# A gated linear attention with a low-rank mixer on one Trainium2 core: first-layer products per chunk, neighbouring chunks' products in joined pieces, and the written order that goes with them

## The chip, the core and the metric

One core of a Trainium2 chip runs the whole program. TensorE multiplies (results go to PSUM), VectorE (DVE), ScalarE (ACT) and GpSimd (POOL) work element by element, and the sync engine (SP) issues most transfers. Each engine works through its own queue in order. The time is device time in microseconds of one execution; shown is the median of three runs, 530.83 us (529.35 to 532.6). One more execution was profiled; all rows of the profile are from it.

## What is computed

Inputs are q, k, v and a complex gate a for 4 batches, 8 heads, 768 steps and 48 channels per head. With the gate's magnitude limited to 0.999, each head keeps a complex state of 48x48:

```python
S = a[t] * S + outer(k[t], v[t])          # a, S complex; k, v real
y[t] = q[t] @ real(S)
```

The heads' y side by side are x (768 x 384 per batch). A mixer follows:

```python
h = (x.T @ U @ V).T                       # over the 768 steps, rank 32
u = x + h
out = u + maximum(u @ w_ch1, 0) @ w_ch2   # 384 -> 1536 -> 384
```

## The kernel before

**Tiling.** The 768 steps of a batch are cut into 6 chunks of 128, so there are 24 chunks, numbered through all batches; two neighbouring chunks are a group for the gates and a pair (`m`) for the mixer. Within a chunk, prefix sums of log magnitude and phase (products with a triangular matrix, lines 777 to 848) turn the recurrence into ordinary products. `prep` weighs q and k with the decays and phases and turns them: up to chunk 5 on TensorE, later by a transfer that transposes.

**A chunk's chain** (`chain`, lines 940 to 1025) has these pieces on TensorE: `products` (L956), k against q, in two halves of 64 steps; `state` (L976), k against v, the chunk's contribution to the state, in two pieces of four heads; `inside` (L1005), the masked k-q products against v; `before(0)` and `before(1)` (L1013), q against the state that came in and against that of the middle. VectorE copies the products through a mask into `AT` (L959) and makes the states `GM` (middle) and `G` (end) from the state products. ScalarE copies the results out to `xo` (L1022, L1024). `state` and `inside` use the array as tiles of 64 by 64; `products` and `before` as tiles of 64 columns over all rows; the mixer's products use the whole array.

**The mixer** (`mixer`) of pair 0 is done partly ahead: its first layer is made from x before the low-rank part is known (`turned`, `up`, 36 products of 256 columns), and `corrected` adds the low-rank part later with weights `more` that come from `ranked` (r is turned, L1116; multiplied with w1, L1124; copied to `more` by ScalarE, L1128). Pair 0's second layer is `down` (L1303), pair 1's first layer `up` (L1102); from pair 2 on the first layer is done with fewer products (`up_fewer`, L1214), and from pair 1 on the second too (`down_two`, L1346). `spread` (L1071) multiplies r with V, `mixed` adds it to xo, `turned` transposes xo into `uT` (L1087, L1091).

**The gates** of a group need the tables for logarithm and exponential first and those for arctangent and sine then; each change is a table load on ScalarE (L463). From chunk 7 on, the phase at the end of a chunk is added to the first row of the next chunk's by a transfer with addition that POOL issues (L828, `gate<-F`); the cast L836 on VectorE waits for it, and the product L842 for the cast.

**The order.** Each piece is entered into a plan with its engine, what it reads and writes, and which buffers it takes. The program is then issued in the order of the list `ORDER`, written out by hand as numbers of the pieces; the plan asserts that no piece comes before what it needs and that no buffer is taken too early. A piece is issued as a whole: nothing of the same engine comes between its instructions. `WARM` puts filler products (L1513, units of 128 columns into a tile that nothing reads) ahead of numbered pieces; before, 33 of them with 52 units. `SPARE` puts single products of 128 columns (L1506) ahead of pieces, into the bank that the piece will overwrite.

**Banks.** Five PSUM banks are shared in rotation by all pieces tagged T or Y: a piece that takes a bank waits until the reader of the bank's last contents is done. State products take two (one for the last chunk of a batch), `inside` and `before` two more.

Weights come as 64-bit numbers and are converted in pieces by VectorE and ScalarE (lines 616 to 625, `stage` and `w`), while the attention part runs.

## Time and profile before

| | |
|---|---|
| median of three runs | 530.83 us |
| profiled execution | 529.77 us |
| its span, first to last instruction | 528.0 us |
| TensorE products busy | 509.3 us (96%), 6670 records |
| VectorE busy | 414.5 us (79%) |
| ScalarE busy | 346.0 us (66%) |
| mean granted TensorE clock | 0.997 |

The span is what the trace shows; 1.77 us of the execution lie around it. A product of 32-bit floats has two records for TensorE (PE) and two for its weight load (PEld), so 12 records are six products. The chain of waits follows the work that ended last back to its start; in it, a row's time runs to the start of what follows, while a row of the timeline runs to the modelled end of its last instruction, which overlaps the next. A wait row gives who waited for whom, the total, how often, and the longest. A row of windows gives the window, its length, then busy time and number of instructions for TensorE, its weight loads, VectorE, ScalarE and GpSimd, the granted clock, the share of the transfer engines and the rate.

### The profile page before, as it was taken

To read this page: it belongs to the slowest core of one execution; us is meant where nothing else is said; L and a number is where in the kernel's file an instruction comes from. 1 tells how busy PE (TensorE), PEld (TensorE's weight loads), DVE (VectorE), ACT (ScalarE), POOL (GpSimd) and SP (SyncE) were. 2 spreads that over 40 slices of the span, in tenths; PEclk is the share of its full clock that TensorE was granted. 3 is DMA by queue.
4 is the path that set the end of the run, shared out by engine and by line. 5 is a ranking of instruction groups with operands and counts; after the bars stand their busy time and mean duration, and the time that the engine had idled before them with its cause. 6 is when DMAs were issued, how large, how long until landed. Compare 5 with 4: busy or idle time off the path is not lost.

```text
span 528.0 us, 15692 instructions
## 1 busy us (share of the span) xinstructions
PE 509.3 (96%) x6670; PEld 460.3 (87%) x6670; DVE 414.5 (79%) x787; ACT 346.0 (66%) x555; POOL 31.6 (6%) x61
## 2 busy tenths in 40 slices
PE   4999999899999999999999999999999999999996
PEld 2777887666998997999999989999999989999996
DVE  4779897799989987898798797878796575958452
ACT  8899998998869978978896768843543313131100
POOL 1000000001010000101011000110000000000110
PEclk9999999999999999999999999999999999999998
DMA  9959958479999998999899958999897543333101
GB/s 226 173 115 270 209 115 191 140 138 217 197 215 244 216 215 145 204 217 202 205 198 227 210 144 175 170 242 229 192 217 178 108 90 61 76 60 61 39 32 35
DMA packets 280670, 87.06 MB, mean 165 GB/s; under 512 B 271288, under 2 KB 272784, under 8 KB 280592
## 3 DMA queue, kind: packets, MB, share of 16 engines
q1 hardware_dynamic: 278384, 81.63, 76.0%
q0 software_dynamic: 2208, 4.35, 2.4%
q8 instruction: 54, 0.88, 0.7%
q14 instruction: 24, 0.20, 0.1%
HBM read 43.03 MB, written 23.63 MB: 126 GB/s over the span
## 4 chain that ended last, share of the span: by engine, by line
PE 88%; ACT 5%; DMA 3%; DVE 2%; issue 1%; SPq 0%; ACTq 0%
PE down L1346 25%; PE few L1214 14%; PE bank L1214 11%; PE up L1102 6%; PE inner L956 4%; PE bank L1013 4%; PE bank L976 4%; PE down L1303 3%; PE bank L1005 2%; DMA gate<-F 2%; PE bank L1071 2%; PE bank L1087 2%; ACT gate L466 1%; PE bank L777 1%; PE bank L782 1%; PE bank L842 1%
## 5 line engine op out<-in xcount | busy, mean ns | idle before, releaser
L466 ACT ACTIVATE gate<-gate 128x768 f32<-128x768 f32 (+2 forms) x85 | 86.1, 1018 | 25.8 <-DMA gate<-in_a_im_dram 14.7
L1346 PE MATMUL down<-w,h 128*128 128x192 f32 x396 | 70.4, 328 | 0.0
L466 ACT ACTIVATE QK<-QKC 128x768 uint16<-128x768 uint16 (+1 forms) x72 | 58.5, 848 | 13.1 <-DVE QKC L469 7.9
L1346 PEld LDWEIGHTS down<-w,h 128*128 128x128 f32 x396 | 64.6, 190 | 1.2 <-issue 0.8
L469 DVE TENSOR_TENSOR QKC<-qk,cs 128x768 f32<-128x768 f32 x48 | 44.9, 952 | 1.0 <-ACT cs L466 0.6
L472 DVE TENSOR_TENSOR xo<-down,xo 128x192 f32<-128x192 f32 (+1 forms) x79 | 29.9, 385 | 14.3 <-PE down L1346 14.1
L1222 ACT COPY h<-few 128x512 f32<-128x512 f32 x35 | 20.2, 583 | 27.8 <-PE few L1214 27.6
L1222 ACT COPY h<-bank 128x512 f32<-128x512 f32 x25 | 14.3, 588 | 36.0 <-PE bank L1214 31.0
L1346 PE MATMUL down<-stage 128*128 128x192 f32 x198 | 37.2, 328 | 0.0
L1102 PE MATMUL up<-uT,w 128*128 128x256 f32 x144 | 33.8, 383 | 0.0
L1346 PEld LDWEIGHTS down<-stage 128*128 128x128 f32 x198 | 32.5, 190 | 0.3 <-issue 0.2
L1102 PEld LDWEIGHTS up<-uT,w 128*128 128x128 f32 x144 | 26.7, 190 | 4.9 <-issue 0.6
L1290 POOL DMA_DIRECT2D out_dram<-xo x32 | 18.5, 590 | 202.9 <-DVE xo L472 164.5
L463 ACT ACT_TABLE_LOAD x22 | 28.2, 1283 | 1.1 <-PEq L1567 0.7
L828 POOL DMA_DIRECT2D gate<-F x15 | 12.0, 797 | 274.7 <-DVE stage L616 86.3
L1226 DVE CUSTOM_DVE_ANT_1 h<-few,h 128x512 f32<-128x512 f32 x31 | 21.0, 686 | 8.8 <-PE few L1214 8.1
L1214 PE MATMUL few<-extra,w 128*128 128x128 f32 x216 | 27.8, 275 | 0.0
L956 PE MATMUL inner<-QK 112*64 112x64 f32 x768 | 27.5, 224 | 0.2 <-DVE AT L959 0.2
L466 ACT ACTIVATE cs<-F 128x384 f32<-128x384 f32 x48 | 24.4, 518 | 3.9 <-DVE F L851 3.7
L956 PEld LDWEIGHTS inner<-QK 112*64 112x64 f32 x768 | 24.5, 138 | 2.4 <-issue 0.8
L1214 PEld LDWEIGHTS few<-extra,w 128*128 128x128 f32 x216 | 26.3, 192 | 0.1
L466 ACT ACTIVATE es<-bank 128x384 f32<-128x384 f32 x44 | 18.4, 502 | 9.2 <-PE bank L777 8.2
(185 smaller groups left out, 1166.8 us busy)
## 6 DMA issues: line engine op xcount, KB each, us to landing
xd<-QK SPq DMA_DIRECT2D x36, 512.0 KB
gate<-in_a_re_dram SPq DMA_DIRECT2D x48, 192.0 KB
gate<-in_a_im_dram SPq DMA_DIRECT2D x48, 192.0 KB
stage<-in_moe_w_ch_dram SPq DMA_DIRECT2D x12, 768.0 KB
qk<-in_q_dram SPq DMA_DIRECT2D x24, 192.0 KB
qk<-in_k_dram SPq DMA_DIRECT2D x24, 192.0 KB
VP<-in_v_dram SPq DMA_DIRECT2D x24, 192.0 KB
out_dram<-xo POOLq DMA_DIRECT2D x12, 192.0 KB, 4.2
```

The source lines that it names most:

```text
L463: ACT(1.37, rank, lambda: nc.scalar.preload_act_table_set(name), writes=[TABLE])
L466: return nc.scalar.activation(out=o, in_=i, func=f, **kw)
L469: nc.vector.tensor_tensor(out=o, in0=a, in1=b, op=OP.mult)
L472: nc.vector.tensor_tensor(out=o, in0=a, in1=b, op=OP.add)
L956: nc.tensor.matmul(out=get(*ps0)[r:r + HC, h], lhsT=k_of(h, r, HC), rhs=q_of(h, r, HC), start=True, stop=True, tile_position=(0, r))
L976: nc.tensor.matmul(out=get(*dk[r])[x:x + D, h], lhsT=get(*ks)[at, h, x // DP, 0:D], rhs=get(*VPi)[at, h], start=True, stop=True, tile_posi ...
L1013: nc.tensor.matmul(out=get(*y[u])[side(r, u), p], lhsT=q_of(h, r * HC, HC), rhs=get(*(mid_G if r else ("G", i - 1)))[:, h], start=False, s ...
L1102: nc.tensor.matmul(out=get(*ps)[:, e], lhsT=w1[:, f, (ff + e) * 128:(ff + e + 1) * 128], rhs=get(*uT)[:, f], start=(f == 0), stop=(f == KD ...
L1214: nc.tensor.matmul(out=get(*ps)[:, q], lhsT=w()[:, q * 128:(q + 1) * 128], rhs=v[0](), start=(n == 0 and q == 0), stop=True, skip_group_ch ...
L1222: ACT(c_act(n3 * CH) - 0.045, RU, lambda i=i, k=k: nc.scalar.copy(out=at(i, k), in_=get(*ps)), [ps], [o])
L1226: DVE(c_dve(n3 * CH), RU, lambda i=i, k=k: nc.vector._custom_dve(dve_ops.TENSOR_ADD_SAT, out=at(i, k), in0=get(*ps), in1=at(i, k), s0=math ...
L1346: nc.tensor.matmul(out=get(*to)[:, part], lhsT=x(j), rhs=y[:, j], start=(first and j == 0), stop=(j == KH - 1), skip_group_check=not first)
```

## The change

There are four parts.

1. Pair 0's first layer is made for each of its two chunks by itself (`up_one`): 72 products of 128 columns for 36 of 256, in 12 pieces as before, with six evacuations of 512 columns as before. Chunk 0's pieces no longer need chunk 1.
2. From `JOIN = 8` on, the chains of neighbouring chunks of a batch are joined, at 14 places. One piece holds all state products of chunk i and the `inside` products of chunk i-1; the next holds the `before` products of chunk i-1 and `products` of chunk i. The end state `G` of chunk i is made behind the second piece, then the masked copy of chunk i and the copies out of chunk i-1. The last chunk of a batch has its `inside` and `before` in pieces of their own. 54 pieces fall away; no product does.
3. `spread` no longer lists a read of `uT`, and `turned` takes the buffer instead.
4. The order is written anew for the new numbers, on all engines. Among other things more of TensorE's work stands between a carry's transfer and its cast at ten of fifteen chunks, the loads of the second gate group stand earlier in SP's queue and the second block of weights later. There are 39 filler products with 55 units and 7 spare products for 4.

The list of the order is cut to its first lines.

```diff
--- before
+++ after
 ORDER = (
-    5, 97, 96, 0, 1, 2, 3, 102, 99, 101, 103, 4, 104, 105, 106, 107, 98, 116, 100, 115, 117, 118, 119, 10, 154, 8, 111, 112, 16, 9, 230, 108, 231,
...
+    5, 97, 96, 0, 1, 2, 3, 4, 99, 102, 101, 103, 104, 105, 106, 107, 100, 8, 98, 111, 10, 151, 230, 231, 153, 9, 154, 108, 109, 115, 116, 112, 117,
...
 )
 SPARE = {
-    410: 3, 447: 1,
+    403: 1, 447: 1, 451: 2, 636: 3,
 }
 
 WARM = {
-    112: (2, 1), 126: (1,), 136: (2, 2, 2, 2, 2, 2, 1), 141: (2,), 162: (2, 2, 2), 235: (2, 2, 2, 2, 1), 242: (2,), 245: (2,), 259: (2, 2, 1), 266: (1, 1, 1, 1, 1, 1, 1, 1, 1),
+    125: (2, 1), 136: (2, 2, 2, 2, 2, 2), 140: (2, 2), 166: (2, 2), 187: (2,), 239: (2, 2, 2, 2, 1, 1, 1, 1, 1, 1, 1, 1, 1), 242: (1, 1, 1, 1, 1, 1, 1, 1, 1, 1, 1, 1, 1),
 }
 
...
@@ -369,6 +367,7 @@
     PARTS = [[(n, n + 1) for n in range(GC)]] + [[g] for g in GROUPS[1:]]
     NG = len(GROUPS)
     AGAIN = range(NG)
+    JOIN = 8
 
     EARLY, SPREAD = 6, (0, 1, 2)
     SPLIT = range(3, NG)
@@ -948,51 +947,44 @@
             return get(*QK)[0:DQ, 1, h * CH + lo:h * CH + lo + n]
 
         ps0 = ("inner", i)
-        psum(ps0, "A", [128, H, HC])
+        last = c == NCH - 1
+        joined, joins = c > 0 and i >= JOIN, not last and i + 1 >= JOIN
+        G, mid_G = ("G", i), ("GM", i)
+        ks, dk = ("qkc", 2 * i + 1), [("dk", (i, r)) for r in range(2)]
+        parts_k = range(1 if last else 2)
+        y, xi = [("y", (i, r)) for r in range(2)], ("xo", i)
+        y_in = [VPi, ATi, mid_G] + ([("G", i - 1)] if c else [])
 
         def products():
             for h in range(H):
                 for r in range(0, CH, HC):
                     nc.tensor.matmul(out=get(*ps0)[r:r + HC, h], lhsT=k_of(h, r, HC), rhs=q_of(h, r, HC), start=True, stop=True,
                                      tile_position=(0, r))
-        PE(0.947, RL, products, [QK], [ps0], takes=[ATi], way=1, steps=4 * H)
-        DVE(0.17 + 0.00104 * H * HC, RL, lambda: nc.vector.copy_predicated(
-            out=get(*ATi), mask=mask.bitcast(I32).unsqueeze(1).to_broadcast([128, H, HC]), data=get(*ps0)), [ps0, ("mask", 0)], [ATi])
-
-        G, mid_G, last = ("G", i), ("GM", i), c == NCH - 1
-        ks, dk = ("qkc", 2 * i + 1), [("dk", (i, r)) for r in range(2)]
-        buffer(mid_G, "GM", 2, [DQ, H, D])
-        if not last:
-            buffer(G, "G", 2, [DQ, H, D])
-        parts_k = range(1 if last else 2)
-        for r in parts_k:
-            psum(dk[r], "Y", [128, H, D], [128, H, DP])
-
-        def state(h0):
-            for h in range(h0, h0 + HH):
+
+        def kept():
+            DVE(0.17 + 0.00104 * H * HC, RL, lambda: nc.vector.copy_predicated(
+                out=get(*ATi), mask=mask.bitcast(I32).unsqueeze(1).to_broadcast([128, H, HC]), data=get(*ps0)), [ps0, ("mask", 0)], [ATi])
+
+        def state(h0, n=HH):
+            for h in range(h0, h0 + n):
                 for r in parts_k:
                     at = slice(r * HC, (r + 1) * HC)
                     for x in (0, DP):
                         nc.tensor.matmul(out=get(*dk[r])[x:x + D, h], lhsT=get(*ks)[at, h, x // DP, 0:D], rhs=get(*VPi)[at, h],
                                          start=True, stop=True, tile_position=(r * HC, x))
-        for h0 in (0, HH):
-            PE(0.443, RR, lambda h0=h0: state(h0), [ks, VPi], [dk[r] + (h0,) for r in parts_k], way=3,
-               steps=4 * HH * len(parts_k),
-               takes=[mid_G] + ([] if last else [G]))
 
         half0, half1 = (lambda r=r: get(*dk[r])[0:DQ] for r in range(2))
-        if c:
-            DVE(c_dve(DM), RR, lambda: add(get(*mid_G), get("G", i - 1), half0()), [("G", i - 1), dk[0]], [mid_G])
-        else:
-            ACT(c_act(DM), RR, lambda: nc.scalar.copy(out=get(*mid_G), in_=half0()), [dk[0]], [mid_G])
-        if not last:
-            DVE(c_dve(DM), RR, lambda: add(get(*G), get(*mid_G), half1()), [mid_G, dk[1]], [G])
-            DVE(c_dve(DM), RR, lambda: mul(get(*G), get(*G), T_of(i)), [("T", group_of(i))], [G])
-
-        y, xi = [("y", (i, r)) for r in range(2)], ("xo", i)
-        for r in range(2):
-            psum(y[r], "Y", [128, HH, D], [128, HH, CH])
-        buffer(xi, "xo", 8, [128, DM])
+
+        def states(first):
+            if not first:
+                pass
+            elif c:
+                DVE(c_dve(DM), RR, lambda: add(get(*mid_G), get("G", i - 1), half0()), [("G", i - 1), dk[0]], [mid_G])
+            else:
+                ACT(c_act(DM), RR, lambda: nc.scalar.copy(out=get(*mid_G), in_=half0()), [dk[0]], [mid_G])
+            if not last and first != joined:
+                DVE(c_dve(DM), RR, lambda: add(get(*G), get(*mid_G), half1()), [mid_G, dk[1]], [G])
+                DVE(c_dve(DM), RR, lambda: mul(get(*G), get(*G), T_of(i)), [("T", group_of(i))], [G])
 
         def side(r, u):
             return slice((r ^ u) * HC, (r ^ u) * HC + HC)
@@ -1013,18 +1005,68 @@
                     nc.tensor.matmul(out=get(*y[u])[side(r, u), p], lhsT=q_of(h, r * HC, HC),
                                      rhs=get(*(mid_G if r else ("G", i - 1)))[:, h], start=False, stop=True,
                                      tile_position=(0, (r ^ u) * HC), skip_group_check=True)
-        PE(0.44, RR, inside, [VPi, ATi, mid_G] + ([("G", i - 1)] if c else []), y, way=3, takes=[xi], steps=4 * H)
+
+        def befores():
+            for r in range(0 if c else 1, 2):
+                before(r)
+
+        def rooms():
+            for r in range(2):
+                psum(y[r], "Y", [128, HH, D], [128, HH, CH])
+            buffer(xi, "xo", 8, [128, DM])
+
+        def halves(a):
+            return a.rearrange("p (a u d) -> p a u d", u=2, d=D)
+
+        def leaves():
+            ACT(c_act(HH * D) - 0.04, RR, lambda: nc.scalar.copy(out=halves(get(*xi))[:, :, 0], in_=get(*y[0])), [y[0]], [xi + (0,)])
+            for r in range(2):
+                ACT(c_act(HH * D) + 0.04, RR, lambda r=r: nc.scalar.copy(out=halves(get(*xi))[r * HC:(r + 1) * HC, :, 1],
+                                                                         in_=get(*y[1])[side(r, 1)]), [y[1] + (r,)], [xi + (r + 1,)])
+        b_in = [QK, mid_G] + ([("G", i - 1)] if c else [])
+        psum(ps0, "A", [128, H, HC])
+        buffer(mid_G, "GM", 2, [DQ, H, D])
+        if not last:
+            buffer(G, "G", 2, [DQ, H, D])
+        for r in parts_k:
+            psum(dk[r], "Y", [128, H, D], [128, H, DP])
+        if joined:
+            p_inside, p_in, p_y, p_befores, p_b, p_leaves, p_rooms, p_takes = pending.pop(i - 1)
+            p_rooms()
+
+            def fused_x():
+                state(0, H)
+                p_inside()
+            PE(1.3, RR, fused_x, [ks, VPi] + p_in, [dk[r] for r in parts_k] + p_y, way=3, steps=4 * H * len(parts_k) + 4 * H,
+               takes=[mid_G] + p_takes)
+            states(True)
+
+            def fused_y():
+                p_befores()
+                products()
+            PE(1.8, RR, fused_y, p_b + [QK], p_y + [ps0], takes=[ATi], way=1, steps=8 * H)
+            states(False)
+            kept()
+            p_leaves()
+        else:
+            PE(0.947, RL, products, [QK], [ps0], takes=[ATi], way=1, steps=4 * H)
+            kept()
+            for h0 in (0, HH):
+                PE(0.443, RR, lambda h0=h0: state(h0), [ks, VPi], [dk[r] + (h0,) for r in parts_k], way=3,
+                   steps=4 * HH * len(parts_k),
+                   takes=[mid_G] + ([] if last else [G]))
+            states(True)
+        if joins:
+            pending[i] = inside, y_in, y, befores, b_in, leaves, rooms, [xi]
+            return
+        rooms()
+        PE(0.44, RR, inside, y_in, y, way=3, takes=[xi], steps=4 * H)
         if c:
             PE(0.467, RR, lambda: before(0), [QK, ("G", i - 1)], [y[0] + (0,), y[1] + (0,)], way=1, steps=2 * H)
         PE(0.467, RR, lambda: before(1), [QK, mid_G], [y[0] + (1,), y[1] + (1,)], way=1, steps=2 * H)
-        def halves(a):
-            return a.rearrange("p (a u d) -> p a u d", u=2, d=D)
-        ACT(c_act(HH * D) - 0.04, RR, lambda: nc.scalar.copy(out=halves(get(*xi))[:, :, 0], in_=get(*y[0])), [y[0]], [xi + (0,)])
-        for r in range(2):
-            ACT(c_act(HH * D) + 0.04, RR, lambda r=r: nc.scalar.copy(out=halves(get(*xi))[r * HC:(r + 1) * HC, :, 1],
-                                                                     in_=get(*y[1])[side(r, 1)]), [y[1] + (r,)], [xi + (r + 1,)])
-
-
+        leaves()
+
+    pending = {}
 
     def mixer(m, ahead=False):
         i0 = m * MC
@@ -1070,7 +1112,7 @@
                         at, c = slice(cc * MC * R, (cc + 1) * MC * R), c0 + cc
                         nc.tensor.matmul(out=get(*ps[cc])[:, y * DH:(y + 1) * DH], lhsT=V[at, c * CH:(c + 1) * CH],
                                          rhs=get(*r)[at, y * DH:(y + 1) * DH], start=True, stop=True, tile_position=(cc * MC * R, 0))
-            PE(0.76, R0, products, [r, ("V", 0)] + [uT + ("kept",)] * (m >= AHEAD), ps, way=5, steps=8)
+            PE(0.76, R0, products, [r, ("V", 0)], ps, way=5, steps=8)
             return ps
 
         def mixed(cc, ps):
@@ -1085,7 +1127,7 @@
             def turn():
                 for f in range(KD):
                     nc.tensor.transpose(out=get(*tr)[:, f], in_=get(*u)[:, f * 128:(f + 1) * 128], identity=ident)
-            PE(0.33, R0, turn, [u], [tr], steps=KD)
+            PE(0.33, R0, turn, [u], [tr], takes=[uT], steps=KD)
             to = lambda: get(*uT)[:, :, cc * CH:(cc + 1) * CH]
             if cc or m >= 3:
                 ACT(c_act(DM) - 0.045, R0, lambda: nc.scalar.copy(out=to(), in_=get(*tr)), [tr], [uT + (cc,)])
@@ -1105,6 +1147,20 @@
                 PE(1.295 * len(es), RM, lambda es=es: products(es), [uT] + [("w1", f, lo) for f in range(KD)], [ps + (e,) for e in es], takes=[h],
                    steps=2 * KD * len(es))
             ACT(c_act(2 * N) - 0.045, R0, lambda: act(get(*h)[:, ff:ff + 2], get(*ps), AF.Copy if ahead else AF.Relu), [ps], [h + (ff,)])
+
+        def up_one(cc, ff):
+            ps = out_of("up", (m, ff, cc), [128, 4, CH], None)
+            at = slice(cc * CH, (cc + 1) * CH)
+
+            def products(es):
+                for e in es:
+                    for f in range(KD):
+                        nc.tensor.matmul(out=get(*ps)[:, e], lhsT=w1[:, f, (ff + e) * 128:(ff + e + 1) * 128],
+                                         rhs=get(*uT)[:, f, at], start=(f == 0), stop=(f == KD - 1))
+            for es in ((0, 1), (2, 3)):
+                PE(1.34, RM, lambda es=es: products(es), [uT + (cc,)] + [("w1", f, lo_) for f in range(KD) for lo_ in sorted({(ff + e) * 128 // WP * WP for e in es})],
+                   [ps + (es[0],)], takes=[h], steps=2 * KD * len(es))
+            ACT(c_act(4 * CH) - 0.045, R0, lambda: act(get(*h)[:, ff:ff + 4, at], get(*ps), AF.Copy), [ps], [h + (ff,), h + (ff + 2,)])
 
         def ranked():
 
@@ -1389,8 +1445,8 @@
         if ahead:
             for cc in range(MC):
                 turned(cc)
-            for ff in range(0, KF, 2):
-                up(ff)
+                for ff in range(0, KF, 4):
+                    up_one(cc, ff)
             return
         if m < AHEAD:
             if c0 == 0:
```

170 rows, old and new, of the table ORDER are left out of this document.

## The prediction

> **What bounds the kernel now.** I read the page first: engines, slices, chain. The rows:
>
> ```profile
> span 528.0 us, 15692 instructions
> PE 509.3 (96%) x6670; PEld 460.3 (87%) x6670; DVE 414.5 (79%) x787; ACT 346.0 (66%) x555; POOL 31.6 (6%) x61
> PE   4999999899999999999999999999999999999996
> PE 88%; ACT 5%; DMA 3%; DVE 2%; issue 1%; SPq 0%; ACTq 0%
> ```
>
> TensorE is busy for 509.3 of 528.0 us and is 88% of the chain that ended last. So a gain must be time taken out of TensorE's stream, or out of the 18.7 us in which it idles. Two windows and TensorE's own waits say where it idles:
>
> ```profile
> 0.00:15.00 15.00, 7.25 (x19) 4.92 (x20) 8.30 (x23) 11.50 (x23) 1.94 (x14) 1.00 0.96 221
> 480.00:528.00 48.00, 43.17 (x306) 42.72 (x304) 24.41 (x58) 4.26 (x7) 3.73 (x7) 0.97 0.13 36
> ...
> PE bank L782 <- DVE GL L742: 7.7, 1, 7.7
> PE up L1142 <- ACT more L1128: 2.1, 1, 2.1
> PE down L1346 <- DVE xo L472: 1.1, 1, 1.1
> PE down L1346 <- DVE stage L1338: 0.7, 1, 0.7
> PE bank L1071 <- ACT r L1054: 0.6, 1, 0.6
> PE bank L976 <- issue: 0.4, 1, 0.4
> ```
>
> 7.7 us pass ahead of the first product and 4.8 us at the end (48.00 less 43.17). Both kernels do the same there. The other long waits are five, of 4.9 us together. In the first 40 us TensorE looks full, but it runs filler products there (the warm products of the spare tile): ScalarE and VectorE make the gates, and the real stream becomes dense with this product:
>
> ```profile
> 43.78 0.91 PE L845 MATMUL bank<-gate,prefix_z 128*128 128x384 f32 x2
> ```
>
> From there to the end TensorE has no filler but four spare products. So three things count: when the dense stream starts, how much work it holds, and how many waits are left in it. Durations are from the profiled execution: 529.77 us, of which 528.0 are span and 1.77 lie around it. It is 1.06 us below the median of the runs shown (530.83). I work out a difference on it and apply that to the median.
>
> **Changes of tile shape.** The joined pieces move no work; they set products of one tile shape next to each other. What a change of shape costs, from the chain:
>
> ```profile
> 335.35 1.08 PE inner L956 x32
> ...
> 337.28 1.09 PE few L1214 x8
> ...
> 339.26 0.89 PE few L1214 x8
> ...
> 346.73 0.95 PE inner L956 x32
> ```
>
> The inner products of a chunk take 1.08 us between other shapes and 0.95 ahead of which the same shape stood: 0.13. Four products of the full array take 1.09 behind a small shape and 0.89 behind their own: 0.20. I counted neighbours of different shape in the two written orders of TensorE's pieces: 143 before, 131 after. Changes to or from the full array are 94 before and 96 after; changes between two small shapes fall from 49 to 35. At about 0.14 for a small pair and 0.17 for one with the full array (half of 0.13 and half of 0.20) that is 14 x 0.14 less 2 x 0.17: **-1.6 us**. Bounds: 12 x 0.13 and 12 x 0.20, -1.6 to -2.4. All of it lies on TensorE's stream.
>
> **The first layer per chunk.** 36 products of 256 columns (12 of the hidden blocks by 3) become 72 of 128 columns. No row has this product with 128 columns, so I take the two next to it, at two records a product:
>
> ```profile
> 54.60 2.59 PE up L1102 x12
> ...
> 446.65 4.47 PE bank L1214 x40
> ...
> L1102 PEld LDWEIGHTS up<-uT,w 128*128 128x128 f32 x144 | 26.7, 190 | 4.9 <-issue 0.6 <-ACT uT L1091 0.2
> ```
>
> Six products of 256 columns take 2.59, 0.432 each: 36 are 15.5 us. Twenty of 128 columns with full weights take 4.47, 0.2235 each: 72 are 16.1 us. **+0.55 us**. The evacuations stay six of 512 columns on ScalarE. Low end: nothing, if chunk 0's products fill a wait. High end: the weight loads. A load record lasts 190 ns and each product has two, so 72 products that waited for their own loads would take 27.4 us, +11.9. I take the low row, since its products have loads of the same size (128x128) and still follow each other at 0.2235.
>
> [...]
>
> **The wait for the ranked weights.** Before, batch 0's rank-side products wait 2.1 us for the copy into `more` (L1128). ScalarE's rows ahead of it:
>
> ```profile
> 88.85 0.46 ACT L1054 COPY r<-rank 128x384 f32<-128x384 f32 x1
> ...
> 91.78 1.10 ACT L466 ACTIVATE stage<-stage 128x768 uint16<-128x768 uint32 x1 [2.04 <-DVE w L472]
> 92.88 1.28 ACT L463 ACT_TABLE_LOAD   x1
> 94.17 0.89 ACT L466 ACTIVATE w<-stage 128x768 f32<-128x768 f32 x1
> 94.96 0.59 ACT L466 ACTIVATE extra<-up 128x512 f32<-128x512 f32 x1
> 95.44 0.48 ACT L1128 COPY more<-bank 128x384 f32<-128x384 f32 x1
> ...
> 89.73 0.74 PE L1116 MATMUL bank<-both,r 64*128 64x32 f32 x5
> ...
> 93.32 0.55 PE L1087 MATMUL bank<-ident,xo 128*128 128x128 f32 x3
> ```
>
> A table load and two conversions of weights stand between the copy of r and this one, and ScalarE idles 2.04 us for VectorE ahead of them. In the new order the same four stand there, but the table load comes directly behind r, into that idle time: 1.28 + 0.89 + 1.10 + 0.59 = 3.9 us, then 0.48. TensorE meanwhile passes the turn of r, its spread and the rank products, from 89.73 to 93.32, and two turns of xo at 0.55 or less each: 4.1 to 4.7 us, so up to 0.3 us of wait is left. The other side: the piece of the first layer that covered the copy of r is gone from its place, and the turn of r waits as the uncovered spread does in the waits above, 0.6. So 2.1 becomes 0.9: **-1.2 us**; bounds -2.1 and 0.
>
> **The carries.** Each chunk's phase total reaches the next chunk through a transfer that POOL issues; the cast behind it (L836) stands in VectorE's queue, and what is behind that waits too. The chain shows two, and VectorE's waits the sum:
>
> ```profile
> 151.00 6.34 DMA gate<-F
> ...
> 275.81 6.09 DMA gate<-F
> ...
> DVE GS L836 <- DMA gate<-F: 4.3, 4, 1.7
> ```
>
> Behind these two the products of the second layer wait 1.1 and 0.7 us (in the waits above: queued behind the cast are the sums `stage` and the additions to `xo`). In the new order TensorE's work between making F and the cast is longer in both places: at chunk 11 a joined piece and one step of the first layer more, at chunk 17 two joined pieces. VectorE's work there is not longer, so its own wait stays, but what TensorE needs next no longer stands behind the cast. Chunk 21 goes the other way, with fewer pieces between. I take **-1.5**; bounds -1.8 and +0.7 (the same wait at a new place).
>
> **The last chunk of a batch.** In batch 1 the joined piece of chunks 10 and 11 ends with chunk 11's inner products, and directly behind it comes what reads their masked copy. Before, the carry-in products of chunk 10 (about 1 us) stood between. The copy's price:
>
> ```profile
> 200.92 1.15 PE L956 MATMUL inner<-QK 112*64 112x64 f32 x32
> 202.12 0.76 DVE L959 COPY_PREDICATED AT<-mask,inner 128x512 f32<-128x512 int32 x1 [0.76 <-PE inner L956]
> 203.02 0.68 PE L1005 MATMUL bank<-VP,AT 64*64 64x48 f32 x32
> 205.44 0.84 PE L976 MATMUL bank<-VP,QKC 64*48 64x48 f32 x56 [0.43 <-issue]
> ```
>
> From 202.07 to 203.02 it is 0.95 us, now open. Against it goes the wait of 0.43 that the state products of chunk 12 have here and that moves behind the spread: **+0.5**; bounds 0 and +0.95. Batches 2 and 3 have at least two pieces of the second layer there.
>
> **The start.** Up to its fourth table load (41.58) ScalarE does the same instructions in both orders, so its idle time decides:
>
> ```profile
> 9.16 0.52 ACT L466 ACTIVATE gate<-gate 128x384 f32<-128x384 f32 x1 [0.45 <-DVE gate L736]
> 14.20 0.87 ACT L466 ACTIVATE es<-bank 128x384 f32<-128x384 f32 x2 [0.94 <-PE bank L782]
> 15.09 1.28 ACT L463 ACT_TABLE_LOAD   x1
> 17.91 0.58 ACT L466 ACTIVATE F<-bank,magic 128x384 f32<-128x384 f32 x1 [0.59 <-PE bank L845]
> 41.58 1.28 ACT L463 ACT_TABLE_LOAD   x1
> ```
>
> The new order puts the first chunk's x into the wait of 0.45 and the second chunk's into that of 0.94; it makes F before the second arctangent, so the wait of 0.59 becomes about 0.9. -0.45 - 0.94 + 0.3 = **-1.1 us**, and the fourth table load comes at about 40.5. With it go the phases that open the dense stream. The gates of chunks 2 and 3 are squared earlier; their four loads move up in SP's queue, ahead of the second block of weights, which moves back. Bounds -1.4 and +1.0 (a load that lands late; nothing before shows one). Filler products rise from 33 to 39; while ScalarE is late they cost nothing, and without that cover some 0.7 us (three more units of 128 columns at 0.2235).
>
> **Spare products**: seven in place of four. One stands in the wait for r. The other two cost 2 x 0.2235 = **+0.45** where TensorE doesn't wait; bounds 0 and 0.7. The later taking of the `uT` buffer and the dropped read in the spread cost nothing: no write carries that name.
>
> **Sum**: -1.6 + 0.55 - 1.2 - 1.5 + 0.5 - 1.1 + 0.45 = -3.9. I allow +0.6 for waits at places I haven't found, since the old order has five of 0.4 to 2.1. That is -3.3: 526.5 on the profiled execution, **527.5 us** on the median.
>
> **Rivals.**
> - *Waits only move.* TensorE's order is rewritten everywhere, so removed waits (2.1, 1.1, 0.7) and the lead at the start may come back elsewhere. Left are -1.6 + 0.55 + 0.45 + 0.5, about 0: 530.7. For it: VectorE is 79% busy and every wait removed hangs on a queue. Against: the places can be named.
> - *More than the sum.* The terms at their good ends (-2.4, 0, -2.1, -1.8, 0, -1.4, 0) give -7.7, 523.1; half-way from the forecast is 525.3.
> - *Joined pieces wait.* A joined piece holds the state products of one chunk and the masked products of the one before, so it can wait for the masked copy. Place: the 14 joins; price 0.95 each, at worst +13.3, about 541. It turns the result slower by over 1% from ten of them on (8.6 us to undo the gain and pass 1%). Against: at every join at least four pieces of the two layers, 0.89 or more each, lie between the inner products and what reads their copy; only chunk 11's unjoined piece has none.
> - *Weight loads bind.* 72 products at 0.38 in place of 0.2235: +11.3 on the forecast, 538.8. The row at 0.2235 leaves little of it. [...]
>
> **Chances.** Forecast 0.55, waits only move 0.20, more than the sum 0.18, joined pieces wait 0.05, weight loads 0.02. About 1% of 530.83, 5.3 us, is what a measurement of this kernel can tell from no change. Faster by that means below 525.5: 0.18 and 0.04 of the forecast's own case, 0.22; slower 0.07; within it 0.71. The range goes from 523.5 to 532, which takes in the first two rivals but for the far end of the gain.
>
> **What would show it.** The second table load near 14 us and the fourth near 40.5; the first dense phase product near 42.7; the wait on `more` below 0.5, with a new one of about 0.6 ahead of the turn of r; the two waits of the second layer behind the carries gone; 1 us of TensorE idle at chunk 11's masked products; first-layer products of 128 columns at about 0.22. It is wrong if these come at 0.38, if TensorE waits at several joins, or if the fourth table load isn't earlier.

## The result: slower by 1.1%

The changed kernel takes **536.0 us** (median of four executions, 535.5 to 536.6) against 530.25 for the kernel before (median of four); the ratio is 1.0107, with a 95% interval of 1.0082 to 1.0131. The forecast was 527.5 with a range up to 532.0: the time lies outside, on the other side. The profiled execution took 535.69 us, 533.9 of them span, against 529.77 and 528.0.

The page of the changed kernel, its span, engines and chain:

```profile
span 533.9 us, 15855 instructions
PE 510.7 (96%) x6760; PEld 464.3 (87%) x6760; DVE 415.7 (78%) x787; ACT 348.1 (65%) x555; POOL 31.7 (6%) x61
PE 84%; ACT 8%; DVE 5%; issue 2%; DMA 1%; SPq 0%; ACTq 0%; DVEq 0%
```

TensorE is as busy in share as before, 96%, but is a smaller part of the chain (84% for 88%), and ScalarE a larger one (8% for 5%). TensorE's own waits in the changed kernel (who waited for whom, total, times, longest):

```profile
PE bank L781 <- DVE GL L741: 8.1, 2, 7.7
PE bank L973 <- issue: 2.4, 1, 2.4
PE bank L1113 <- ACT r L1096: 1.9, 1, 1.9
PE up L1562 <- DVE extra L1204: 1.3, 2, 0.8
PE bank L997 <- DVE AT L965: 0.9, 1, 0.9
PE bank L997 <- DVE GM L471: 0.6, 1, 0.6
PE bank L776 <- DVE GS L760: 0.6, 1, 0.6
PE down L1402 <- DVE h L1282: 0.5, 1, 0.5
...
PE bank L1172 <- ACT r L1096: 0.2, 1, 0.2
```

The three waits that the change was to remove (2.1 on `more`, 1.1 and 0.7 behind the carries) are gone. In their place stand others, and the longest names no engine: 2.4 us ahead of a state product (L973), put down to "issue". Windows of the kernel before (first fence) and of the changed one (second), from the first dense product to the end and in two stretches (length, then busy time and number of instructions by engine, granted clock, share of the transfer engines, rate):

```profile
43.78:528.00 484.22, 474.35 (x6224) 435.03 (x6222) 384.48 (x731) 307.20 (x493) 29.69 (x47) 1.00 0.78 163
60.00:75.00 15.00, 14.96 (x310) 12.66 (x300) 12.86 (x20) 14.84 (x25) 0.00 (x0) 1.00 0.76 173
200.00:220.00 20.00, 18.93 (x365) 16.77 (x360) 15.48 (x33) 17.78 (x32) 2.15 (x3) 1.00 0.79 157
```

```profile
44.11:533.90 489.79, 476.18 (x6304) 439.11 (x6300) 388.45 (x736) 308.59 (x493) 29.79 (x47) 1.00 0.75 161
60.00:75.00 15.00, 12.60 (x318) 11.97 (x313) 10.70 (x17) 11.07 (x19) 0.00 (x0) 0.89 0.88 190
200.00:220.00 20.00, 16.49 (x371) 13.59 (x368) 15.19 (x26) 17.03 (x32) 1.95 (x3) 1.00 0.88 187
69.10:72.50 3.40, 3.02 (x42) 2.92 (x42) 2.10 (x3) 0.01 (x1) 0.00 (x0) 0.50 0.72 163
```

The 5.9 us by which the span grew are 0.33 of a later start (44.11 for 43.78), 3.74 of idle time behind it (489.79 less 476.18, against 484.22 less 474.35) and 1.83 of busy time. Two stretches hold most of it. Between 60 and 75 us TensorE idles 2.4 us, and right behind, for 3.4 us, its granted clock is 0.50. At the end of batch 1, between 200 and 220 us, it idles 3.5 us in place of 1.1.

What the 2.4 us are is not in any wait. The timeline of the changed kernel (start, length, engine, line, idle time before):

```profile
66.51 0.57 PE L973 MATMUL bank<-VP,QKC 64*48 64x48 f32 x32
...
69.48 0.89 PE L973 MATMUL bank<-VP,QKC 64*48 64x48 f32 x32 [2.40 <-issue]
```

Both rows are chunk 3's state products: the two pieces read the same tiles and write the same two banks, so that what the second needs, the first had. The page has one more row that I had passed over, the queue that brings instructions:

```profile
q8 instruction: 55, 0.90, 0.7%
```

These are 55 packets of 16 KB. TensorE's records in the trace, 6760 products, 6760 weight loads and 71 semaphore instructions, are 13591. The two idle times of the dense stream that are put down to "issue", 0.27 us at 46.47 and 2.40 at 69.48, stand at records 962 and 1730, 768 apart, and the one of the kernel before, 0.43 us at 205.44, at record 5570, 3840 behind 1730. 768 and 3840 are 3 and 15 times 256, and 13591 is 53.1 times 256, near the number of packets. The theory from here on: **TensorE's program comes in blocks of 256 records, and at 67.1 us the next block wasn't there yet.** The rivals: something else stops TensorE in those microseconds; the first layer's 72 products cost more than their row showed; the start is to blame; the waits in batch 1 are. In what follows "the end of a block" is a record whose number, counted in the trace, is 194 more than a multiple of 256; the product at 69.48 is number 1730 = 6 x 256 + 194. A "hole" is idle time of TensorE ahead of such a record.

### The profile page after: what moved, and what is told of

The parts are those of the page before. It is cut to its first block, busy times and chain, and to the rows that moved or that the text cites. A ratio compares the mean times of both kernels' runs of the same rounds, so it can differ in the third digit from the quotient of the medians.

```text
span 533.9 us, 15855 instructions
## 1 busy us (share of the span) xinstructions
PE 510.7 (96%) x6760; PEld 464.3 (87%) x6760; DVE 415.7 (78%) x787; ACT 348.1 (65%) x555; POOL 31.7 (6%) x61
## 4 chain that ended last, share of the span: by engine, by line
PE 84%; ACT 8%; DVE 5%; issue 2%; DMA 1%; SPq 0%; ACTq 0%; DVEq 0%
PE down L1402 27%; PE few L1270 13%; PE bank L1270 11%; PE bank L1005 4%; PE inner L961 4%; PE bank L973 3%; PE up L1158 3%; PE up L1144 3%; PE down L1359 3%; ACT gate L465 3%; PE bank L997 2%; PE bank L1113 2%; PE bank L1129 2%; PE bank L781 2%; PE bank L841 1%
## 5 line engine op out<-in xcount | busy, mean ns | idle before, releaser
L1346 POOL DMA_DIRECT2D out_dram<-xo x32 | 19.9, 657 | 172.1 <-DVE xo L471 118.9
L973 PEld LDWEIGHTS bank<-VP,QKC 64*48 64x48 f32 x1408 | 19.8, 123 | 9.0 <-issue 6.5
L961 PE MATMUL inner<-QK 112*64 112x64 f32 x768 | 27.2, 224 | 0.2 <-PE bank L1005 0.2
L961 PEld LDWEIGHTS inner<-QK 112*64 112x64 f32 x768 | 24.5, 138 | 1.1 <-PE bank L1005 0.3
L973 PE MATMUL bank<-VP,QKC 64*48 64x48 f32 x1408 | 22.9, 209 | 2.4 <-issue 2.4
L1270 PE MATMUL bank<-extra,w 128*128 128x128 f32 x184 | 24.1, 275 | 0.0
```

The lines of the kernel that those rows point to most:

```text
L961: nc.tensor.matmul(out=get(*ps0)[r:r + HC, h], lhsT=k_of(h, r, HC), rhs=q_of(h, r, HC), start=True, stop=True, tile_position=(0, r))
L973: nc.tensor.matmul(out=get(*dk[r])[x:x + D, h], lhsT=get(*ks)[at, h, x // DP, 0:D], rhs=get(*VPi)[at, h], start=True, stop=True, tile_posi ...
L1270: nc.tensor.matmul(out=get(*ps)[:, q], lhsT=w()[:, q * 128:(q + 1) * 128], rhs=v[0](), start=(n == 0 and q == 0), stop=True, skip_group_ch ...
L1346: queue.dma_start(out=out[b, c * CH:(c + 1) * CH, lo:hi], in_=get("xo", i)[:, lo:hi])
```

## The experiments

Differences are in medians against the kernel before, as measured beside each kernel; to be compared with +5.75 for the changed kernel. Where only the order is altered, the diff shows the moved numbers of `ORDER` between their new neighbours.

**The hole covered (e1).** Pieces 341 and 340 are chunk 3's state products, 285 and 296 first-layer pieces.

```diff
 338
-341
-340
 285
 296
+341
+340
 287
```

> The changed kernel, with the two state pieces of chunk 3 placed behind two first-layer pieces (12 products of 128 columns) that stood behind them; nothing else is moved. Theory A (TensorE had used up the instructions it holds, in a stretch of small products, and the next block of them came late): the first-layer pieces take 2.7 us with 48 records, the block arrives meanwhile, the idle 2.4 us between the two state pieces fall below 0.5, the granted clock between 60 and 75 us stays at 1.00, and the total falls by 2.4 + 1.3 = 3.7 us against the changed kernel, to +2.0 us on the kernel before. Theory B (something else stops TensorE from 67.1 to 69.5 us, a transfer or the clock): about 2.4 us of idle time in the same microseconds, now ahead of other products; total +5.7 us as the changed kernel. Theory C (the block is asked for only when TensorE has none left): the same 2.4 us between the same pieces, 2.7 us later; total +5.7 us.

534.18 against 530.93 (ratio 1.0060, 1.0035 to 1.0084): +3.25 in place of +5.75. The timeline where the hole had been, of this kernel:

```profile
66.30 2.94 PE L1158 MATMUL up<-uT,w 128*128 128x128 f32 x24
69.17 1.11 PE L973 MATMUL bank<-VP,QKC 64*48 64x48 f32 x64
```

Both state pieces run through in one row, and the clock stays at 1.00 from 60 to 75 us. Theory A holds and B and C fall: the same microseconds hold no idle time, and neither does the place between the two state pieces, 2.7 us later. The gain is 2.5 us where 3.7 were expected. For the clock I had expected 1.3; the busy time behind the start is 475.30 here against 476.18, so it was about 0.9. The 2.4 us of this hole went, but the idle time behind the start fell by 1.8 only, from 13.61 to 11.84: short waits came, 0.4 us of them put down to "issue" again, ahead of `products` (L961).

**Other transfers out of the way (e11).** TensorE's program stays; 57 is a block of weights, 377 and 376 are k and q of chunk 5, 29 is a copy of V, 195, 196 and 63 are other loads; SP's pieces alone are shown.

```diff
 195
-57
-377
-376
 29
 196
+57
+377
+376
 63
```

> The changed kernel with three transfers of 0.77 and 0.38 MB together (a block of weights, q and k of chunk 5) issued 5 us later by SP, behind the second copy of V and two small loads; in the changed kernel they are issued from 62.8 to 64.4 us, just ahead of the packet of instructions that started 3.0 us behind the time at which TensorE entered the block (66.89 against 63.88). TensorE's program is the same. If the packet waits in the transfer engines behind those three: it starts within 1.5 us, the 2.4 us of idle time fall to 1 or less, and the clock stays; total 1.4 to 3 us below the changed kernel, +2.7 to +4.3 us on the kernel before. If its wait has nothing to do with them: the same 2.4 us, +5.7 us or more, as the weights come later.

533.51 against 530.80 (1.0042, 1.0023 to 1.0062): +2.7, the good end of the first expectation. In the changed kernel TensorE enters the block that ends at 1730 at 63.88 us. A view of the transfers from there to 66.85 us has no packet of instructions (first line below: packets, MB, share of the transfer engines); the view from 66.85 to 69.48 has one (second line):

```profile
q1 hardware_dynamic: 374, 0.80, 92.7%
...
q8 instruction: 1, 0.02, 2.1%
```

In this kernel TensorE enters the block at 64.56, and the packet comes between 65.16 and 65.90. The window of this kernel:

```profile
60.00:75.00 15.00, 15.00 (x401) 14.25 (x402) 12.62 (x21) 14.58 (x21) 0.00 (x0) 1.00 0.87 186
```

No idle time at all, though SP still issues all three loads within these 15 us. So the packet had waited 3.0 us, in which 0.80 MB of other transfers went; with the three loads (1.15 MB) out of its way it waits 0.6 us, and the block is there in time. This one change of SP's order gives back about half of the loss. It isn't free of its own: the end of a block at record 962, at 47 us, costs 0.65 us here and 0.27 in the changed kernel.

**The kernel before, shifted (e5).** The sharpest test takes the change out altogether: 28 products of one column at the very start of the kernel before, where TensorE has nothing to do.

```diff
 WARM = {
+    111: (0,) * 28,
...
     def warm(u):
...
+        if u == 0:
+            nc.tensor.matmul(out=spare[0][0:1, 0, 0:1], lhsT=ident[:, 0:1], rhs=ident[:, 0:1], start=True, stop=True)
+            return
```

> The kernel before, with 28 products of one column by one column into the spare tile at the very start, where TensorE idles 7.7 us anyway; they are read by nobody, and all else is as it was. Each has two records and two of its load, so everything behind stands 112 records later in TensorE's program. Theory A (TensorE's program comes in blocks of 256 records; a block comes 2.3 to 2.9 us behind the start of its packet, and the packet starts when the block before it is entered, or up to 4 us later where transfers queue; the ends of the blocks fall on records 194 more than a multiple of 256): the ends of the blocks now fall into stretches of small products, near 43, 65, 185 and 203 us; worked out from the trace of before with the waits of the packets seen so far, 8 to 15 us of idle time in place of 1, in the middle 10.9; the total +7 to +13 us, about 541. Theory B (the idle times belong to the work itself, not to where the blocks end): within 0.5 us of the kernel before.

537.29 against 531.01 (1.0119, 1.0079 to 1.0160): **+6.3 us for work done in idle time**, as much as the whole change costs. The expected middle was +10 and the low end +7, so the size was overrated; of the four places two were right (43 and 65 us). Windows of this kernel from the start to just ahead of the first product behind four of its holes, then its waits:

```profile
0.00:64.32 64.32, 54.62 (x731) 40.34 (x732) 47.37 (x85) 56.21 (x99) 1.94 (x14) 1.00 0.90 187
0.00:71.06 71.06, 58.11 (x859) 43.30 (x860) 49.51 (x88) 61.30 (x103) 1.94 (x14) 1.00 0.90 194
0.00:91.36 91.36, 77.80 (x1241) 59.61 (x1242) 64.73 (x111) 77.39 (x131) 1.94 (x14) 0.98 0.76 165
0.00:98.10 98.10, 83.16 (x1369) 63.55 (x1370) 69.18 (x119) 82.92 (x141) 2.44 (x15) 0.98 0.78 170
```

```profile
PE bank L977 <- issue: 3.3, 1, 3.3
...
PE bank L1006 <- issue: 1.7, 1, 1.7
...
PE rank L1049 <- issue: 1.4, 1, 1.4
PE up L1103 <- issue: 0.8, 1, 0.8
```

731 + 732 products and weight loads are done at the hole of 64.32, 859 + 860 at that of 71.06: 256 apart. The same at 91.36 and 98.10. (The counts leave out TensorE's semaphore instructions, 10 and then 14; with them the records behind the holes are 1474, 1730, 2498 and 2754.) Four different kinds of product, one spacing.

**The first layer per chunk alone (e3), and shifted (e6).** e3 is part 1 of the change (with the buffer names of part 3) in the old order:

```diff
-            for ff in range(0, KF, 2):
-                up(ff)
+                for ff in range(0, KF, 4):
+                    up_one(cc, ff)
```

> The kernel before with the first part of the change alone: the first pair's first layer per chunk, its pieces at the old places one by one (one piece moved behind three others, since it needs the second block of weights earlier), no joined pieces, the old order else. By the prediction's term: +0.55 us. If products of 128 columns cost more than their row showed, through weight loads or through instructions (72 in place of 36): +2 us or more, and TensorE idle behind nothing that the profile shows, in the stretch of chunks 2 to 5. If the second block of weights is late: a wait on its conversion of 0.5 us or more ahead of the fourth piece.

541.03 against 530.93 (1.0176, 1.0138 to 1.0215): **+10.1 us**. Its waits (line numbers are 3 higher than in the changed kernel):

```profile
PE bank L976 <- issue: 4.6, 3, 3.6
PE up L1201 <- ACT more L1187: 2.1, 1, 2.1
PE rank L1093 <- ACT stage L468: 1.8, 1, 1.8
PE bank L1093 <- ACT cs L468: 1.8, 1, 1.8
PE inner L964 <- issue: 0.8, 1, 0.8
PE up L1161 <- DVE w L474: 0.7, 1, 0.7
```

The second and third expectations both show. The 0.7 is the second block of weights. The two waits of 1.8 are put down to ScalarE, but the records behind them are 2754 and 5826, both ends of blocks, and in e6 below, where 112 records more move these ends, neither wait is there: the profile names the last semaphore, and here that was not the cause. Part 1 adds 144 records, which moves every later end of a block by more than half a block. e6 tests that with the 28 products of e5 ahead, 144 + 112 = 256:

> The first layer per chunk alone in the old order, as in the earlier run, with the same 28 products of one column at the start. The first layer per chunk has 144 records more than the old one, so with 112 more ahead of it every block behind it ends where it ends in the kernel before (144 + 112 = 256). Theory A (the ends of the blocks): the idle times of 3.6, 0.8, 1.8, 1.7 and 0.9 us that came with the first layer per chunk go, and what stays is its own price, 0.55 us by the prediction's term and 0.7 for its wait on the second block of weights: +0.5 to +2 us on the kernel before, 9 us below the same kernel without the 28 products. Theory B (72 products of 128 columns cost 10 us of themselves): +10 us, as before.

536.41 against 531.01 (1.0099, 1.0068 to 1.0130): +5.4. The same 28 products that cost the kernel before 6.3 us make this one 4.6 faster, so theory B falls as it stands. But it isn't the +0.5 to +2 that I expected. What is left, from the waits of this kernel and a window:

```profile
PE up L1201 <- ACT more L1187: 2.1, 1, 2.1
PE bank L976 <- issue: 1.6, 1, 1.6
...
PE bank L1000 <- issue: 1.3, 1, 1.3
PE up L1161 <- DVE w L474: 0.7, 1, 0.7
```

```profile
90.00:120.00 30.00, 27.87 (x186) 19.66 (x181) 21.44 (x36) 23.46 (x36) 0.96 (x1) 0.89 0.67 132
```

Inside the stretch that holds the new products (up to 95 us) the ends of the blocks are still off by up to 112 records, and one of the waits put down to "issue" stands there, 1.6 us at 68.83; the other long one is 1.3. The 0.7 for the weights stays. And the wait on `more`, as long as in the kernel before (2.13 for 2.10), is followed by a low clock, which it isn't there (1.00 from 90 to 120 us): 0.89 in the mean of 30 us would be 6.6 us at the 0.50 of the changed kernel, an estimate.

**The start (e4).** The order of the kernel before up to the phases of chunk 3, the new one from there.

```diff
-    5, 97, 96, 0, 1, 2, 3, 4, 99, 102,
+    5, 97, 96, 0, 1, 2, 3, 102, 99, 101,
...
-    125: (2, 1), 136: (2, 2, 2, 2, 2, 2), 140: (2, 2),
+    112: (2, 1), 126: (1,), 136: (2, 2, 2, 2, 2, 2, 1),
```

> The changed kernel with the order of the kernel before on all engines up to the phases of chunk 3 (about 47 us), filler products included, and the new order from there. If the new start costs only what its first dense product shows (44.11 against 43.78): 0.3 us below the changed kernel, +5.4 us on the kernel before. If the start's order of the loads is what bunches the transfers between 60 and 70 us, where TensorE idles 2.4 us: that time and the lower clock behind it go too, +2 us on the kernel before.

537.32 against 530.93 (1.0126, 1.0077 to 1.0175): +6.4, not to be told from the changed kernel. The first dense product comes at 43.89, 0.2 us earlier. The idle time at record 1730 is still there (2.1 us, without a low clock behind it: 1.00 from 60 to 75 us), with two others at ends of blocks (0.45 at 91 us, 1.2 at 383 us): six filler products fewer, 24 records, moved them. The order of the start's loads is not what makes the hole; what the old start is worth by itself can't be told from this total, since the ends of blocks moved with it.

**The end of batch 1 (e2, e8, e7).** 891 and 893 are the joined pieces of chunks 10 and 11, 1155 the phase piece of chunk 14, 573 a piece of the second layer, 898 chunk 11's `inside`, 905 the copy of r, 1186 a turn of cos and sin. e2:

```diff
+891
 1155
...
-891
 893
+573
 898
...
+905
 1186
...
-905
```

> The changed kernel with three pieces moved at the end of batch 1: the joined piece of chunks 10 and 11 stands ahead of the two phase pieces of chunks 14 and 15, one second-layer piece (6 products) stands behind the second joined piece, where the masked copy of chunk 11 is waited for, and ScalarE copies r ahead of the last two turns of cos and sin of chunk 13. If the waits there are what batch 1 loses: the wait for AT (0.92) goes, that for r falls from 1.94 to about 1.0, total 1.9 us below the changed kernel, +3.8 us on the kernel before. If the waits only move (VectorE's cast and sum of the log magnitudes, waited for 0.95 us in the changed kernel, are then waited for longer): no gain, +5.7 us.

540.18 against 530.93 (1.0167, 1.0121 to 1.0212): +9.3, worse than either expectation, by 3.5 us or more.

```profile
PE bank L997 <- ACT xo L1022: 2.3, 1, 2.3
...
PE bank L1129 <- DVE xo L471: 0.9, 1, 0.9
PE bank L1113 <- ACT r L1096: 0.6, 1, 0.6
```

The wait for r fell to 0.6. But chunk 11's `inside` now waits 2.3 us for a bank that ScalarE empties late, and the clock is 0.83 between 200 and 220 us. e8 moves the copy of r alone:

> The changed kernel with the copy of r in batch 1 placed on ScalarE ahead of the last two turns of cos and sin of chunk 13, nothing else. If ScalarE's queue alone makes the wait: it falls from 1.94 to about 0.9 and the total by 1.0 us, to +4.7 us on the kernel before. If what is behind it takes the time back (the weighted q and k of chunk 13 are made later, and the state products of chunk 12 stand behind them): no gain, +5.7 us.

535.61 against 531.01 (1.0102, 1.0066 to 1.0137): +4.6, which can't be told from +5.75. In the trace the wait for r goes from 1.9 to 0.6, and two others come behind it: 0.9 for `xo` ahead of the turns, 0.6 ahead of pair 3's first layer. So the wait mostly moves. e7 puts e1's order, e8's and four filler products fewer (`242: (1,) * 9`) together:

> The changed kernel with three repairs: the state pieces of chunk 3 behind two first-layer pieces (as tried), four filler products fewer at about 25 us (16 records, so that the blocks end a little earlier in all that follows), and the copy of r in batch 1 ahead of two turns of cos and sin on ScalarE. By what was measured and worked out: 2.5 us less for the first, 0.6 for the second (idle time at the ends of blocks 0.9 in place of 1.5), 1.0 for the third: 4.1 us below the changed kernel, +1.6 us on the kernel before. If the waits only move: 2.5 us below the changed kernel.

533.95 against 531.01 (1.0058, 1.0039 to 1.0076): +2.9, which is e1's gain and little more. Ahead of `before` products (L1005) three waits put down to "issue" take 0.6, 0.9 and 0.4 us, for one of 0.27 in the changed kernel: by theory A the 16 records less moved ends of blocks into them.

**The joins alone (e10).** `JOIN = 8` in the old order with the old first layer.

```diff
+    JOIN = 8
```

> The second part of the change alone: the 14 joins, in the old order (a joined piece at the place of the last of its parts, and what depends on it behind it), the old first layer and the old start. Neighbours of different tile shape fall from 143 to 127 on TensorE. By the prediction's price of 0.14 for a change between small shapes and 0.17 for one with the full array: 2.2 to 2.7 us less, 528.5. If a change of shape costs less than that, or the pieces of the full array lose what the small ones win: within 1 us of the kernel before. If the longer stretches of small products run out of instructions (64 records in 0.5 us; the ends of the blocks stay where they are but for the moved pieces), or the joined pieces wait: +1 to +4 us, and the idle time stands at records 194 more than a multiple of 256, or ahead of joined pieces.

560.08 against 530.80 (1.0541, 1.0518 to 1.0564): +29 us, far above all three. The longest of some twenty waits:

```profile
PE bank L841 <- DVE GM L471: 4.0, 2, 2.8
PE few L1270 <- ACT h L1278: 3.1, 2, 2.4
PE bank L973 <- DMA VP<-in_v_dram: 2.7, 1, 2.7
```

The joins hold back what depended on their parts; in an order not made for them they cost 29 us. So this run tells nothing about the price of a change of shape; that the joins alone gain anything was not shown.

**Two removed waits by themselves (e9, e12).** The change removed the wait on `more` and those behind the carries. Both can be had in the kernel before by ScalarE's and VectorE's order alone, with TensorE's program as it was. e9 (621 is the table load, 406 the copy into `more`, 294 the evacuation, 78 and 77 conversions):

```diff
+621
 78
-621
+406
+294
 77
-294
-406
```

> The kernel before with ScalarE's order changed at one place: the table load that stands behind the second conversion after r moves ahead of that conversion, into the 2.0 us in which ScalarE idles there, and the copy into more and the evacuation next to it move ahead of the other conversion. Nothing of TensorE's program changes. By the prediction's working of the wait on more: it falls from 2.1 to 0.3 us or less, and the total by 1.8 to 2.1 us, to 529.0, if nothing gives it back. If a later wait takes it (the second layer behind the first carry, 1.1 us in the kernel before, waits for a transfer that doesn't come earlier): 1.0 us less in the total.

**528.81 against 530.80** (0.9970, 0.9952 to 0.9987): -2.0, as worked out; this version beats both kernels. In e12 the cast 757 and the sum 758 also go behind 476 and 480:

```diff
-757
-758
 476
 480
+757
+758
```

> The kernel before with the repair of the wait on more, as tried, and one more of VectorE's order: at chunk 11 the cast that waits for the carry's transfer, and the sum behind it, stand behind the two sums that the second layer needs next (stage and xo), which stood behind them. Nothing of TensorE's program changes. By the prediction's reading of the carries (what TensorE needs stands behind the cast that waits): the wait of 1.4 us of the second layer goes, the cast comes at the same time, and the total falls by 2.0 + 1.4 = 3.4 us, to 527.4. If the wait is the transfer's own, or the next phase product is late because of the cast: 2.0 us less, 528.8.

528.67 against 530.05 (0.9967, 0.9945 to 0.9990): nothing that can be told beyond e9. TensorE's waits in it:

```profile
PE bank L1006 <- issue: 1.2, 1, 1.2
PE few L1215 <- DVE xo L473: 0.6, 1, 0.6
PE bank L1072 <- ACT r L1055: 0.6, 1, 0.6
```

The wait of 1.4 (at 157.70 us in e9) is gone as the reading said, and 0.6 comes back ahead of `few`, at 163.67. But in this profile the end of a block at record 1730, in `inside` (L1006), costs 1.2 us at 70 us, where e9's profile has no wait; so the 0.7 that should be left of the gain can't be seen in the total.

## Why the prediction was wrong

The sum said -3.3 and the span grew by 5.9. Term by term (each with its forecast):

- **The waits not found (+0.6)** is the step that failed most: its +0.6 was taken from the waits of the old order, with no working of where new ones would come. The largest is the block at record 1730: 2.4 us, and 0.9 through the clock. e1, e5 and e11 show the cause: from 63.88 to 67.1 us a stretch of small products uses up its 256 records before the next block comes; at this place the packet of instructions also started 3.0 us after TensorE entered the block before, behind 0.80 MB of other transfers (0.6 us in e11). The 144 records of the new first layer are enough for it: e3 has the hole at the same record in the old order, 3.6 us long. The prediction had a row of it and misread it: the 0.43 ahead of the state products of chunk 12 in the kernel before is record 5570 = 21 x 256 + 194, and not a wait of those products, so it couldn't "move behind the spread".
- **First layer per chunk (+0.55)**: as products, the difference was right. In the timelines its 72 products stand in eight rows of 17.9 us together in e1, and the 36 of the kernel before in eight rows of 17.4 (0.25 and 0.48 each, where I had read 0.22 and 0.43). What the step left out is that 144 records are a cost of their own, on everything behind them: 10.1 us in the old order alone, 5.4 when the later blocks are put back.
- **Wait on `more` (-1.2)**: right and underrated; 2.1 went, 0.2 came ahead of the turn of r. e9 gives 2.0 for it alone.
- **Carries (-1.5)**: both waits went, as read. What the gain is stays open: 0.5 for `h` came in the second layer, and e12, which removes the larger one alone, is no faster than e9, with a hole that hides up to 1.2 us.
- **Last chunk of a batch (+0.5)**: the copy that lies open costs 0.9, as priced. Not seen were the neighbours. ScalarE copies r behind two turns and a conversion, which costs 1.9 (in the kernel before it stood idle for 0.47 ahead of that copy, and the wait was 0.6), and the sum GS is late by 0.6. 200 to 220 us has 2.4 us more idle time, not 0.5. e2 and e8 show that moving single pieces there only moves the waits; a full rearrangement wasn't tried.
- **The start (-1.1)**: wrong, the dense stream begins later and not earlier. Rows of the changed kernel:

```profile
10.64 0.49 ACT L465 ACTIVATE es<-bank 128x384 f32<-128x384 f32 x1 [0.80 <-PE bank L781]
...
17.76 0.58 ACT L465 ACTIVATE F<-bank,magic 128x384 f32<-128x384 f32 x1 [1.00 <-PE bank L844]
...
41.37 1.28 ACT L462 ACT_TABLE_LOAD   x1
```

  One of the two waits that I let go came back as 0.80 on the phase products. The fourth table load is 0.2 earlier, not 1.1, and the dense stream begins 0.33 later; with the old start, in e4, 0.11 later.
- **Spare products (+0.45)**: three more at 0.22 are 0.7, but 1.3 us of waiting stand ahead of three of the seven (`extra`, in the waits above); the kernel before has no such wait.
- **Changes of tile shape (-1.6)**: the busy time behind the start grew by 1.83. Taking off 0.5 for the first layer, 0.7 for the spare products and 0.9 for the clock leaves -0.3. No run measured it by itself, so why so little came of -1.6 stays open.

Read this way, the hole with its clock (3.3), the first layer (0.5), the wait on `more` (-1.9), the carries (-1.3), the end of batch 1 (2.4), the start (0.3), the spare products (2.0) and the shapes (-0.3) make +5.0 of the 5.9 us; the other 0.9 lies in short waits.

Of the rivals, "waits only move" was right about the waits: 4.9 us went, and 1.9 + 1.3 + 0.9 + 0.6 + 0.5 = 5.2 came. "Joined pieces wait" showed at no join; the one wait for a masked copy is at chunk 11's unjoined piece, which the sum had priced. "Weight loads bind" didn't show: 12 products take 2.94, 0.245 each and not 0.38. The case that happened was in none of them. With e11, about 3.0 of the 5.75 us are shown by taking them away; the rest is read from the waits, and no run took it away.

## What to carry to other kernels

A stretch of many small instructions can have a price that no duration shows. Here the program itself came in packets, one for 256 records, and where one started 3.0 us after the block before was entered, behind 0.80 MB of other transfers, TensorE idled 2.4 us; so count records between slow instructions, and look at what is transferred there. An edit that adds or drops instructions shifts the ends of all later blocks: 112 records ahead of everything cost the kernel before 6.3 us (1.2%, e5) and gained 4.6 (0.9%) on e3 (e6), with no work changed. Shift a kernel by half a block of idle instructions before believing in a difference of that size. Where a wait can be removed by reordering the engine that is waited for, try that first and leave the bottleneck's program alone: it gave 2.0 us in e9, though in e8 most of the wait only moved.

## What the runs showed of the hardware

- **Blocks of instructions.** The changed kernel has 55 packets of 16 KB in the queue `q8 instruction` for 13591 records of TensorE, the kernel before 54 for 13405. In the changed kernel the first 52 pair one by one with the 52 records that are 194 more than a multiple of 256: they start from 4.3 us ahead of their record to 3.2 us behind it. In these two kernels every idle time of TensorE from 0.15 us up that is put down to "issue" stands at such a record: 0.27 us at 46.47 and 2.40 at 69.48 in the changed kernel, 0.43 at 205.44 in the one before. They end 2.3, 2.6 and 2.9 us after the packet of instructions starts, and the packet starts 3.2, 3.0 and 1.3 us after TensorE enters the block before. For the block that ends at record 1730 it is 3.0 us in the changed kernel and 0.6 in e11, where three loads are issued later. Five more idle times counted in e3, three in e4 and six in e5 stand at such records too; the longest is 3.6 us, at record 1730 in e3. A chunk's state products are 128 records in 0.9 us. From 302.79 to 305.61 us in the kernel before, 256 records pass in 2.8 us without idle time; there the packet starts at 301.85, 0.9 us ahead of the block before.
- **The clock.** Behind the hole of 2.4 us the granted clock is 0.50 from 69.1 to 72.5 us, 3.4 us, and then 1.00 at once. In e8 a hole of the same length at the same record leaves it alone:

```profile
60.00:75.00 15.00, 12.60 (x320) 12.05 (x316) 10.34 (x16) 12.39 (x19) 0.00 (x0) 1.00 0.88 190
```

  The other runs differ at like idle times too. From 60 to 75 us, with the hole at record 1730, the mean clock is 0.89 in the changed kernel and in e2 (2.4 us each) and in e3 (3.6), and 1.00 in e4 (2.1). From 90 to 105 us, with the wait of 2.1 on `more`, it is 1.00 in the kernel before and 0.87 in e6. From 200 to 220 us, with the wait of 1.9 for r, it is 1.00 in the changed kernel, e1 and e4, and 0.91 in e11. What decides between them was not shown.
